# PSUM banks given out by the schedule in a fused Nyström attention and squared-ReLU MLP kernel: all eight banks in four tiles, one buffer for the squares, a stored table of priorities, the first inverse's last steps side by side

## The chip, the cores and the metric

The kernel runs on one core of one Trainium2 chip. The metric is the device time in microseconds (us) of one execution. The kernel before takes 254.74 us, the median of three runs (254.6 to 255.81). Names of engines: PE is TensorE (PEld its weight loads), ACT is ScalarE, DVE is VectorE, POOL is GpSimd, SP is SyncE.

## The reference, cut to what matters

```python
# q, k, v: (8, 8, 576, 64); w_in: (512, 2048); w_out: (2048, 512)
q_lm, k_lm = means of 18 consecutive rows of q and k          # 32 landmarks
A, Bm, C = sm(q, k_lm), sm(q_lm, k_lm), sm(q_lm, k)           # softmaxes
Z = Bm^T / (norms of Bm)
for _ in range(6):
    Z = 2 * Z - Z @ Bm @ Z                                    # iterated inverse
x = A @ Z @ C @ v                                             # -> (4608, 512)
h = x @ w_in;  r = maximum(h, 0);  out = (r * r) @ w_out      # -> (4608, 512)
```

## The kernel before

The kernel folds Z, C and v into w_in (G = (Z C v) w_in for each of the eight batches), so the MLP's first product is AT,G. Each step is an `Op` with an engine, a duration, what it reads and writes, and the PSUM banks that it takes. A list scheduler in the kernel orders all Ops by a model of the chip, and the program is emitted in that order. There are eight banks of 512 f32 columns. The kernel before has three rings: "h", two tiles of two banks each, and "n" and "o", two tiles of one bank each. Every entry of a ring is a tile of its own to the framework:

```python
RINGS = {"h": 2, "n": 2, "o": 2}

def bank(tag, key, shape, dt=F32):
    PS[key] = psum.tile(shape, dt, tag=tag, bufs=Plan.RINGS[tag], name=tag)
    return PS[key]
```

The two dense steps, with their evictions (cut):

```python
def in_mm(e, hk=hk, f=f):                  # h <- AT,G: two banks of 288 columns
    t = bank("h", hk, [P, 2, 512])
    ...
# ACT: r = relu(h), 576 columns over both banks, in one instruction;  DVE: gT = r * r
# PE:  o += gT[f]^T w_out[f], 16 steps of 512 columns into one bank of ring "o"
# ACT or DVE: osb = copy of that bank;  SP: store
```

The softmax here doesn't subtract the row's maximum and nothing guards it: scores larger than these inputs give would overflow.

## Time and profile before

| | kernel before |
|---|---|
| time, median | 254.74 us |
| span from first to last instruction | 253.2 us |
| PE busy | 95% |
| last quarter of w_in lands, its G group starts | 30.82, 30.86 us |
| last matmul ends | 249.6 us |

First, the shares of the chain that ended last:

```profile
PE 77%; DMA 9%; DVE 6%; POOL 3%; issue 2%; ACT 1%; POOLq 0%
```

ACT has 1%: PE almost never waits for an eviction. Second, the end of the timeline, with start, length, engine, line, operation, tiles and count:

```profile
241.19 8.40 PE L1112 MATMUL o<-w_out_bf,gT 128*128 128x512 bf16 x54
...
243.12 0.58 ACT L323 COPY o<-o 128x512 f32<-128x512 f32 x1 [3.40 <-PE o L1112]
...
246.68 0.58 ACT L323 COPY o<-o 128x512 f32<-128x512 f32 x1 [2.98 <-PE o L1112]
248.15 0.37 ACT L323 COPY o<-o 128x256 f32<-128x256 f32 x1 [0.88 <-PE o L1112]
```

PE runs 8.40 us of output matmuls without a gap, while ACT copies out the bank just finished three times. PE writes the other bank of the ring meanwhile.

### The profile page before, as it was taken

How to read it: one execution, taken by the hardware profiler on the slowest of the kernel's cores; microseconds unless marked ns; L12 is line 12 of the kernel's file. 1: busy time of each engine (PE TensorE's matmuls, PEld its weight loads, DVE VectorE, ACT ScalarE, POOL GpSimd, SP SyncE). 2: the span in 40 equal slices, each digit the busy share in tenths (PEclk: the TensorE clock that was granted, in tenths of full speed). 3: DMA queues.
4: the chain of work that ended last, by engine and by line, in shares of the span. 5: the costliest groups of instructions: out<-in, count | busy, mean ns of one | idle time of the engine just before them, and what ended most of it. 6: DMA issues, size and time to landing. Idle time of an engine off the chain costs nothing.

```text
span 253.2 us, 6580 instructions
## 1 busy us (share of the span) xinstructions
PE 239.9 (95%) x2666; PEld 143.9 (57%) x2701; DVE 174.4 (69%) x487; ACT 164.3 (65%) x282; POOL 29.1 (11%) x51
## 2 busy tenths in 40 slices
PE   8776999999999999999999999999999999999994
PEld 7553775456644656565645565467466644565453
DVE  2774789769966898799897799979866762253000
ACT  3586898567832887677865985679688744474211
POOL 7822200012003000300220030010000000000000
PEclk9995999999999999999999999999999999999999
DMA  7999999999999999799599949997110131301233
GB/s 145 192 206 205 204 206 206 163 165 185 196 112 218 147 229 166 133 202 225 110 159 230 197 58 220 196 177 134 44 41 3 44 83 41 85 0 41 85 83 83
DMA packets 57054, 35.59 MB, mean 141 GB/s; under 512 B 29760, under 2 KB 52544, under 8 KB 57024
## 3 DMA queue, kind: packets, MB, share of 16 engines
q0 software_dynamic: 22672, 18.06, 47.6%
q1 hardware_dynamic: 34352, 17.11, 33.2%
q8 instruction: 21, 0.34, 0.5%
q14 instruction: 9, 0.07, 0.1%
HBM read 36.70 MB, written 9.44 MB: 182 GB/s over the span
## 4 chain that ended last, share of the span: by engine, by line
PE 77%; DMA 9%; DVE 6%; POOL 3%; issue 2%; ACT 1%; POOLq 0%
PE o L1112 39%; PE h L315 12%; PE h L1044 11%; DMA w_in_bf<-in_moe_w_in_dram 8%; PE o L1099 6%; PE h L982 2%; DVE gT L1058 2%; PE n L842 1%; PE n L794 1%; PE n L890 1%; DVE G L325 1%; POOL w_in_bf L397 1%; POOL qraw L390 1%; ACT r L1055 1%; DVE o L325 1%
## 5 line engine op out<-in xcount | busy, mean ns | idle before, releaser
L1112 PE MATMUL o<-w_out_bf,gT 128*128 128x512 bf16 (+1 forms) x494 | 125.1, 372 | 1.9 <-issue 0.6
L1055 ACT ACTIVATE r<-h 128x576 bf16<-128x576 f32 x128 | 78.8, 651 | 20.9 <-PE h L315 18.7
L1058 DVE TENSOR_TENSOR gT<-r 128x576 bf16<-128x576 bf16 x128 | 56.6, 452 | 20.2 <-ACT r L1055 18.2
L1112 PEld LDWEIGHTS <-gT 128*128 128x128 bf16 x528 | 48.1, 98 | 39.2 <-issue 6.0
L1044 PE MATMUL h<-AT,G 128*128 128x288 bf16 x256 | 67.1, 288 | 0.8 <-DVE G L325 0.4
L315 PE MATMUL h<-AT,G 128*128 128x288 bf16 x256 | 67.0, 288 | 0.0
L323 ACT COPY o<-o 128x512 f32<-128x512 f32 (+1 forms) x27 | 15.4, 570 | 35.7 <-PE o L1112 26.4
L315 PEld LDWEIGHTS <-G 128*128 128x128 bf16 x256 | 25.2, 98 | 12.3 <-issue 0.3
L1044 PEld LDWEIGHTS <-G 128*128 128x128 bf16 x256 | 25.1, 98 | 11.4 <-DVE G L325 1.3
L323 ACT CAST G<-h 128x1024 bf16<-128x1024 f32 x17 | 17.2, 1018 | 6.4 <-PE h L982 5.4
L325 DVE CAST G<-h 128x1024 bf16<-128x1024 f32 x13 | 15.9, 1222 | 7.3 <-PE h L315 6.4
L483 POOL COPY gate<-qT 1x1 bf16<-1x1 bf16 x6 | 1.9, 316 | 124.1 <-DMA qT<-qraw 102.9
L807 DVE SCALAR_TENSOR_TENSOR st<-st,n 128x128 bf16<-128x128 bf16 x35 | 9.9, 284 | 7.6 <-PE n L794 7.6
L1099 PE MATMUL o<-w_out_bf,gT 128*64 128x512 bf16 x64 | 14.6, 380 | 0.0
L1101 PE MATMUL o<-w_out_bf,gT 128*64 128x512 bf16 x64 | 14.6, 380 | 0.0
L935 ACT ACTIVATE Ra<-h 128x576 f32<-128x576 f32 x16 | 10.3, 652 | 3.9 <-PE h L315 3.7
L462 DVE TENSOR_TENSOR Pd<-st,ones_d 128x256 bf16<-128x256 bf16 x42 | 12.1, 288 | 0.9
L946 DVE TENSOR_TENSOR AT<-Ea,Ra 128x576 bf16<-128x576 bf16 x16 | 11.7, 753 | 1.2 <-ACT Ra L939 1.2
L849 ACT ACTIVATE EC<-n 96x512 bf16<-96x512 f32 x21 | 12.0, 609 | 0.6 <-PE n L842 0.6
L923 ACT ACTIVATE Ea<-h 128x576 bf16<-128x576 f32 x16 | 9.9, 659 | 3.9 <-PE h L824 3.9
L794 PEld LDWEIGHTS <-Pd 128*128 128x128 bf16 x84 | 7.9, 97 | 6.9 <-DVE Pd L462 1.4
L1099 PEld LDWEIGHTS <-gT 128*64 128x64 bf16 x64 | 6.7, 110 | 7.1 <-issue 1.3
(174 smaller groups left out, 286.8 us busy)
## 6 DMA issues: line engine op xcount, KB each, us to landing
vraw<-in_v_dram POOLq DMA_DIRECT2D x8, 576.0 KB, 7.9
out_dram<-o SPq DMA_DIRECT2D x23, 192.0 KB, 2.5
kraw<-in_k_dram POOLq DMA_DIRECT2D x7, 576.0 KB, 10.1
qraw<-in_q_dram POOLq DMA_DIRECT2D x7, 576.0 KB, 13.4
out_dram<-o SPq DMA_DIRECT2D x24, 128.0 KB, 2.4
w_in_bf<-in_moe_w_in_dram POOLq DMA_DIRECT2D x4, 512.0 KB, 15.2
w_out_bf<-in_moe_w_out_dram POOLq DMA_DIRECT2D x4, 512.0 KB, 21.7
out_dram<-o SPq DMA_DIRECT2D x23, 64.0 KB, 2.2
```

Of the source, the lines that this page charges most:

```text
L315: nc.tensor.add_instruction(mybir.InstMatmult(start_tensor_calc=start, stop_tensor_calc=stop, is_transpose=transpose, ldweights=False, til ...
L323: nc.scalar.copy(dst, src)
L325: ENG[e].tensor_copy(dst, src)
L462: nc.vector.tensor_tensor(dst[:], src.unsqueeze(2).to_broadcast([P, 2, NG, M]), ones_d[:].unsqueeze(1).to_broadcast([P, 2, NG, M]), ALU.mult)
L849: nc.scalar.activation(EC[:, x, :, :, :, :].rearrange("p c i g m -> p (i g) c m"), PS[sc][0:TP, :, :].rearrange("p y (c m) -> p y c m", c= ...
L946: add(("DVE", dve_ns(S)), lambda e, i=i: nc.vector.tensor_tensor(AT[:, i, :], Ea[:, i, :, :].rearrange("p c t -> p (c t)"), Ra[:, i, :, :] ...
L1044: (again if j else nc.tensor.matmul)(t[:, j, 0:HALF], lhsT=G[:, i, f * P:(f + 1) * P], rhs=AT[:, i, j * HALF:(j + 1) * HALF], start=(i == ...
L1055: add(("ACT", act_ns(S)), lambda e, hk=hk, r=r: nc.scalar.activation(r.rearrange("p (j t) -> p j t", j=2), PS[hk][:, :, 0:HALF], AF.Relu), ...
L1058: add(("DVE", dve_ns(S, 2)), lambda e, r=r, f=f: nc.vector.tensor_tensor(gTs[z][:, f, :], r[:], r[:], ALU.mult), reads=[("r", rn)], writes ...
L1099: nc.tensor.matmul(t[0:64, :], lhsT=gTs[0][:, f, 4 * P:S], rhs=w_out_bf[:, f, :], start=(f == 0), stop=(f == NF - 1))
L1101: nc.tensor.matmul(t[64:P, :], lhsT=gTs[1][:, f, 0:64], rhs=w_out_bf[:, f, :], start=(f == 0), stop=(f == NF - 1))
L1112: nc.tensor.matmul(PS[ok][:, 0:hi - lo], lhsT=gTs[z][:, f, x0:x0 + P], rhs=w_out_bf[:, f, lo:hi], start=(f == f0), stop=(f == f1 - 1))
```

## The change

Its intent: let the schedule give out the eight banks freely (up to three two-bank tiles, three "n" and three "o" at a time, any that fit), replace 700 random rounds at build time by a stored table of annealed priorities, keep the squares of two batches in one buffer so that the row tiles that straddle two batches need one matmul per step, run the last steps of the first inverse side by side, and set dummy matmuls at more places of the front end. The diff, cut to what the argument touches (the table, most of the first inverse and the order of loads are left out):

```diff
-    RINGS = {"h": 2, "n": 2, "o": 2}
+    KINDS = {"h": (3, 2), "n": (3, 1), "o": (3, 1)}
+    NBANKS = 8
...
+    def take(self, rn, t, busy):
+        if self.KINDS[rn][1] == 2:
+            b = next(b for b in range(0, self.NBANKS, 2) if max(busy[b], busy[b + 1]) <= t)
+            return (b, b + 1)
+        return (min((busy[b ^ 1] <= t, busy[b], b) for b in range(2, self.NBANKS) if busy[b] <= t)[2],)
...
-    def bank(tag, key, shape, dt=F32):
-        PS[key] = psum.tile(shape, dt, tag=tag, bufs=Plan.RINGS[tag], name=tag)
+    pairs = [psum.tile([P, 2, 512], F32, name="ps%d" % i) for i in range(Plan.NBANKS // 2)]
+
+    def bank(key, shape, dt=F32):
+        b = plan.place[key]
+        t = pairs[b[0] // 2]
+        ...
+        if len(b) == 1:
+            ...
+            t = t[:, b[0] % 2, 0:n]
...
-            blocks((A, "u", 5), Ys[4], us[0], yk(4) + [("u", 4)], at(0.44), busy=1, dim=D)
+            blocks((A, "yy"), Ys[4], Ys[5], yk(4) + yk(5), at(0.42))
...
-    gTs = [sb.tile([P, NF, S], BF16, name="gT%d" % i) for i in range(2)]
+    gT = sb.tile([P, NF, 2 * S], BF16, name="gT")
...
-        end, log = self.search(700)
+        end, log = self.schedule(self.shifts(len(self.ops)))
```

## The prediction

> **What bounds the kernel now.** I first read the busy shares and the slices: PE is at 95% and at 9 in every slice from the fourth to the last but one, so TensorE is the bound, and only the ends are loose. In the slices PEclk falls to 5 once, in the fourth (19 to 25 us), and DMA is at 9 from the second slice on.
>
> ```profile
> PE 239.9 (95%) x2666; PEld 143.9 (57%) x2701; DVE 174.4 (69%) x487; ACT 164.3 (65%) x282; POOL 29.1 (11%) x51
> ...
> PE   8776999999999999999999999999999999999994
> ...
> PEclk9995999999999999999999999999999999999999
> DMA  7999999999999999799599949997110131301233
> ```
>
> Then the chain of work that ended last, in its first 50 us. The first batch's attention is not on it. It consists of the issuing of loads, then the fourth quarter of w_in, which lands at 30.82, and the G matmul that uses it, 0.04 us later; from there on it is PE.
>
> ```profile
> 9.65 0.71 POOL w_in_bf L397
> 10.37 20.45 DMA w_in_bf<-in_moe_w_in_dram
> 30.82 0.04 issue
> 30.86 0.41 PE h L982 x8
> ```
>
> So I cut the span there. Columns: stretch, its length, then busy us of PE, PEld, DVE, ACT, POOL, clock, DMA share, GB/s.
>
> ```profile
> 0.00:31.00 31.00, 24.12 (x483) 18.41 (x484) 18.28 (x72) 19.49 (x37) 14.98 (x29) 0.89 1.16 190
> 31.00:249.50 218.50, 215.66 (x2191) 125.51 (x2217) 156.16 (x416) 144.47 (x245) 14.10 (x22) 1.00 0.78 135
> 249.50:253.20 3.70, 0.09 (x1) 0.00 (x0) 0.00 (x0) 0.37 (x1) 0.00 (x0) 1.00 0.29 81
> ```
>
> Before 31 us PE idles 6.9 us, but the DMA engines never do. From 31 to 249.5 PE idles 2.8 us. The last 3.7 us are the last copy and store. Time = 30.8 (load) + dense PE work + 3.7; the time exceeds the span by 1.5 us (254.74 against 253.2).
>
> A finer look at the dense part, in the timeline of PE: a 512-column matmul starts 216 ns before its successor (median of 441 pairs). Where the successor uses another tile shape of the array it is longer: 39.92 to 40.23 and 41.02 to 41.33.
>
> ```profile
> 39.92 0.38 PE L1112 MATMUL o<-w_out_bf,gT 128*128 128x512 bf16 x1
> 40.23 0.56 PE L890 MATMUL n<-v,EC 96*32 96x65 bf16 x48
> ...
> 41.02 0.38 PE L1112 MATMUL o<-w_out_bf,gT 128*128 128x512 bf16 x1
> 41.33 0.44 PE L824 MATMUL h<-qT,kdup 64*32 64x288 bf16 x16
> ```
>
> Over 15 such pairs the median is 309 ns, so a change of tile shape costs 309 - 216 = 93 ns; after a 288-column matmul it is 216 - 123 = 93 ns too.
>
> **What the Trainium skill says.** "TensorEngine Tiling (Array Packing)", Key Properties: changing the tiling mode, not just the tile, drains TensorE. The trace agrees and gives the price, 93 ns. "TensorE: Matmul & The Clock Gate", Part 1: the clock is at half or full, decided over windows of about 3.4 us of activity. The trace has one half-clock stretch, 18.6 to 25.5 us, 6.83 us or two such windows. The same page, Part 2, says that weight loads are pulled ahead of matmuls in flight. The trace agrees: eight loads for the second half of a G pair are issued at 48.54 to 48.57, and their matmuls start at 48.74, right behind the first half's (48.52); the "no weight load" form of before still shows loads here. So splitting the G pairs into separate instructions should cost nothing. "PSUM — Partial Sum Buffer", Specifications: eight banks of 2 KiB; before fixes them as rings (two double banks, two and two single), after allots the same eight freely.
>
> **The change part by part.**
>
> *First inverse.* The chain at the start, in the timeline of PE:
>
> ```profile
> 19.47 0.29 PE L657 MATMUL n<-cvb,Z4T 32*32 32x64 bf16 x8
> 20.49 0.29 PE L657 MATMUL n<-u,Y 32*32 32x64 bf16 x8 [0.73 <-DVE u L325]
> 21.17 0.25 PE L970 MATMUL h<-Y,u 32*64 32x32 bf16 x8 [0.39 <-DVE u L664]
> 21.88 0.63 PE L982 MATMUL n<-w_in_bf,WT 64*32 64x512 bf16 x8 [0.45 <-ACT WT L323]
> ```
>
> The step u,Y (20.49 to 21.17, 0.68 us) goes; a product Y4 Y5 is made beside the other branch instead. The order of after also puts q's second means before its transposes (0.5 us earlier) and gives the C·v sums their own bank, so that they don't wait for the exponential that reads the shared one (a 0.17 us wait at 16.48). But v is now loaded after the first quarter of w_in: 14.04 becomes about 16.6, since a quarter takes 2.5 us (landings at 28.19 and 30.82). My estimate for the first G matmul is 20.3 in place of 21.88. This 1.5 us does not reach the end by itself: the same ten loads stand before w_in's fourth quarter, in another order, and DMA is saturated, so it still lands at about 30.8.
>
> *Work moved ahead of that landing.* This does reach the end. I counted PE's instructions in the program of each kernel, from the first G matmul to the last group of G of batch 0. Before has 24 of AT,G (288 columns, 122.5 ns) and 36 pairs of means and transposes of k and q (69 ns); after has 28 and 48. That is 4 x 0.1225 + 12 x 0.069 = 1.32 us more, less 0.11 us of one fold that comes later: 1.2 us. It fits: the second-to-last quarter of w_in lands at 28.2, then G 0.3, four matmuls 0.5 and 24 k pairs 1.65 end at 30.75. ACT has seven relus of 0.65 us to do in that time, which it can.
>
> *Both squares in one buffer.* The 64-row tiles of four batch pairs were done as two 128x64 matmuls per step; now it is one of 128x128. 64 steps of about 217.5 ns become 64 of 216: 0.1 us. Their tile shape no longer changes.
>
> *Tile shape changes.* In the two programs, from the first G on: 65 before, 57 after, 8 x 0.093 = 0.75 us.
>
> *Sum.* With each kind's spacing, PE's work from the last G group on is 216.3 us before and 214.35 after: 1.95 us less (1.2 + 0.75). Before took from 30.86 to the last matmul's issue at 249.4, 218.5 us, so 2.2 us were stalls and gaps; the single ones that I find without a missing record are 0.1 to 0.3 us each, about 1.5 us in all. Free banks (three double, three and three single at most) and an annealed order may save a third to a half: I take 0.7. Gain 2.65 us, less 0.3 for the rivals below: 254.74 - 2.35 = 252.4 us.
>
> **The rivals.**
> 1. *The front end pays in full.* If the load did not bind, G at 20.3 would add 1.5 us: about 250.9. The chain of waits speaks against it: 0.04 us between landing and use.
> 2. *The clock goes to half again, now later.* PE has only some 5.5 us of work from 20.3 to 28.2, and the stretch from 15.2 to 18.6, 73% busy, was followed by half clock. If 28.9 to 32.3 ran at half clock, the 24 k pairs (69 to about 107 ns) and AT,G matmuls would cost about 1.4 us: 253.8. For warmth speak the added dummy matmuls (13 more), but they stand before 22 us. I give it three in ten.
> 3. *A new wait for v of batch 1.* It is loaded behind all of w_out now: 30.8 + 4 x 2.5 + 2.9 = 43.8, plus the DVE copy of 0.95 us, against its use on PE, which my count puts at 45.0. Before it landed at 38.74, use at 40.23. A late copy could cost up to 1 us: 253.4.
> 4. *Banks do nothing,* because PE hardly waits for them: 253.1.
>
> **Range and chances.** 1 alone reaches 250.9; 2 and 3 together 254.5. Eight in ten: 250.8 to 254.0. Faster by over 2% needs 249.65, thus 5.1 us, of which the dense part cannot give more than 1.95 + 2.2 and the load's landing hides the rest: 0.06. Slower by over 2% would need a race of stalls that nothing here shows: 0.01.
>
> **What would show it right or wrong.** The last quarter of w_in should land at 30.5 to 31.2 us, with its G matmul right behind; the first G matmul near 20.3; PE's last matmul near 247.2; the tail 3.7; a change of tile shape still 93 ns. Wrong: the last G group well after its load (2, or ACT late); w_in landing by 29 us (1); a PE gap of over 0.5 us at 44 to 47 (3); stalls after 31 us that grow above 2.2 us, or a longer tail.

## More of the kernel before

The framework puts in the semaphore waits by itself. It orders accesses of different engines that overlap on a tile: a matmul that writes a tile waits for the copy that still reads it.

## The result, and the profile after

| | before | after |
|---|---|---|
| time, median of four runs | 255.28 us (254.60 to 257.01) | 286.39 us (285.51 to 287.44) |
| span of the profiled run | 253.2 us | 285.3 us |
| last quarter of w_in lands | 30.82 us | 30.64 us |
| the last G group of batch 0 starts | 30.86 us | 37.62 us |
| last matmul ends | 249.59 us | 281.64 us |

The four runs of the kernel before are the three named at the start and one more. The ratio is 1.1209, 95% interval 1.1133 to 1.1285. Ratios in this document are the mean time of one kernel's fast runs over that of the other's fast runs of the same rounds, so not quite the ratio of the medians quoted. One slow run of the kernel before (258.76 us, in the rounds of x1 to x3) is left out of the ratios.

The changed kernel is 12% slower, far outside the predicted range. Its page, in the order of the prediction's first fence, with the chain's shares last:

```profile
PE 251.2 (88%) x2621; PEld 145.9 (51%) x2658; DVE 174.2 (61%) x479; ACT 166.3 (58%) x287; POOL 28.9 (10%) x51
...
PE   7777889789989988899998899998987997899984
...
PEclk9975999999999999999999999999999999999999
...
PE 70%; DVE 13%; ACT 9%; issue 4%; DMA 2%; another core or an unknown queue 0%; DVEq 0%; ACTq 0%; POOLq 0%
```

The loss is not in one place. The row of PE, which was all 9 from the fourth slice on, has 7s and 8s to the end, and in the chain DVE and ACT have gone from 7% together to 22%. The stretches (columns as in the prediction), cut at the last G group and at the last matmul:

```profile
31.00:37.62 6.62, 4.65 (x90) 3.54 (x88) 3.39 (x8) 3.67 (x7) 0.00 (x0) 1.00 1.24 207
37.62:281.64 244.02, 222.13 (x2101) 124.71 (x2134) 155.47 (x410) 146.47 (x248) 14.01 (x22) 1.00 0.65 116
281.64:285.30 3.66, 0.00 (x0) 0.00 (x0) 0.00 (x0) 0.37 (x1) 0.00 (x0) 0.88 0.15 42
```

The front end is 6.76 us later (37.62 against 30.86), although the load that had set it landed when expected. The dense part takes 244.02 us in place of 218.73 (30.86 to 249.59), 25.3 us more. Together that is 32.1 us, the whole difference of the spans. The tail, 3.66 us, is as before.

What does PE wait for? The waits of the output matmuls (total us, times, longest), where the kernel before had only four "issue" waits of 0.6 us together:

```profile
PE ps L1178 <- ACT o L387: 5.9, 9, 0.7
...
PE ps L1178 <- DVE o L389: 1.8, 3, 0.8
PE ps L1178 <- DVE st L881: 1.7, 5, 0.4
```

An output matmul reads gT and w_out. It needs nothing of `st`, which is a step of another batch's inverse, nor of `o`, the copy of a finished output tile. The timeline at a place like the one shown of the kernel before:

```profile
269.76 1.24 PE L1178 MATMUL ps<-w_out_bf,gT 128*128 128x512 bf16 x5
...
271.04 0.58 ACT L387 COPY o<-ps 128x512 f32<-128x512 f32 x1 [3.95 <-PE ps L1178]
...
271.68 4.70 PE L1178 MATMUL ps<-w_out_bf,gT 128*128 128x512 bf16 x21 [0.67 <-ACT o L387]
...
274.68 0.58 ACT L387 COPY o<-ps 128x512 f32<-128x512 f32 x1 [3.05 <-PE ps L1178]
```

PE ends a tile, ACT copies it (0.58), and only then does PE begin the next tile, though that lies in another bank. The next copy, at 274.68, falls inside 4.70 us of matmuls that do not stop. So it depends on which banks the two tiles have. The front end shows the same:

```profile
16.39 0.22 PE L731 MATMUL ps<-Z,Y 32*32 32x32 bf16 x8 [0.23 <-ACT EC L923]
...
17.02 0.22 PE L731 MATMUL ps<-Y 32*32 32x32 bf16 x8 [0.41 <-ACT EC L923]
```

These are steps of the inverse, the longest chain at the start, waiting for an exponential of C, of which they read nothing.

The built program explains it. In the framework's record of dependences, a wait of this kind reads (matmul into the second bank of ps1, copy out of the first):

```
InstMatmult -> InstTensorCopy (sync): tensor overlap on 'ps1_64' (WAR)
```

I matched every wait of PE on ACT or DVE in the program with the instruction awaited. In the kernel before none is for an instruction that touches only another bank. In the changed kernel 92 are (41 on ACT, 51 on DVE), each between the two banks of one two-bank tile. I call them false waits below: the data need no such order, and they come from tiles, not from banks. Of the stalls that I could match to the program after 31 us, 23.8 us in all, 20.4 us in 40 stalls stand at false waits alone.

The Trainium skill bears on whether the chip needs such a wait: "PSUM — Partial Sum Buffer", section "PSUM bank collisions raise a hardware error", has the rule "Semaphore-guard PSUM by bank × quadrant (by bank is the simple version), not by address." The kernel before agrees: during 8.40 us of matmuls into one bank or the other, ACT read the bank that PE was not writing, three times. A two-bank tile is a coarser guard than a bank.

### The profile page after: what moved, and what is told of

Read it like the earlier page. It is cut to its first block, busy times and chain, and to the rows that moved or that the text cites. A ratio compares the mean times of both kernels' runs of the same rounds, so it can differ in the third digit from the quotient of the medians.

```text
span 285.3 us, 6505 instructions
## 1 busy us (share of the span) xinstructions
PE 251.2 (88%) x2621; PEld 145.9 (51%) x2658; DVE 174.2 (61%) x479; ACT 166.3 (58%) x287; POOL 28.9 (10%) x51
## 4 chain that ended last, share of the span: by engine, by line
PE 70%; DVE 13%; ACT 9%; issue 4%; DMA 2%; another core or an unknown queue 0%; DVEq 0%; ACTq 0%; POOLq 0%
PE ps L1178 39%; PE ps L379 11%; PE ps L1122 9%; ACT o L387 3%; DMA kraw<-in_k_dram 2%; PE ps L1060 2%; ACT r L1134 2%; DVE gT L1137 2%; ACT EC L923 1%; PE ps L916 1%; PE ps L868 1%; DVE st L881 1%; DVE AT L1021 1%; DVE o L1192 1%; PE ps L898 1%
## 5 line engine op out<-in xcount | busy, mean ns | idle before, releaser
L1178 PE MATMUL ps<-w_out_bf,gT 128*128 128x512 bf16 (+1 forms) x557 | 143.8, 373 | 18.3 <-ACT o L387 5.9
L1134 ACT ACTIVATE r<-ps 128x576 bf16<-128x576 f32 x128 | 76.5, 658 | 13.7 <-PE ps L379 9.8
L1122 PE MATMUL ps<-AT,G 128*128 128x288 bf16 x256 | 66.6, 288 | 1.0 <-DVE G L389 0.3
L379 PE MATMUL ps<-AT,G 128*128 128x288 bf16 x256 | 66.5, 288 | 0.0
L387 ACT COPY o<-ps 128x512 f32<-128x512 f32 (+1 forms) x30 | 17.0, 571 | 56.4 <-PE ps L1178 52.2
L387 ACT CAST G<-ps 128x1024 bf16<-128x1024 f32 (+2 forms) x22 | 19.5, 941 | 6.3 <-PE ps L1060 6.3
L389 DVE CAST G<-ps 128x1024 bf16<-128x1024 f32 (+2 forms) x14 | 14.9, 1067 | 11.6 <-PE ps L1060 9.9
L881 DVE SCALAR_TENSOR_TENSOR st<-st,ps 128x128 bf16<-128x128 bf16 x35 | 10.0, 285 | 17.7 <-PE ps L868 11.9
L923 ACT ACTIVATE EC<-ps 96x512 bf16<-96x512 f32 x24 | 13.5, 594 | 3.0 <-PE ps L916 2.4
L1010 ACT ACTIVATE Ra<-ps 128x576 f32<-128x576 f32 x16 | 10.3, 648 | 5.3 <-PE ps L379 5.1
L1060 PE MATMUL ps<-w_in_bf,WT 64*32 64x512 bf16 (+1 forms) x264 | 10.6, 390 | 0.4 <-ACT qpad L387 0.4
```

Source lines behind the costliest of these rows:

```text
L379: nc.tensor.add_instruction(mybir.InstMatmult(start_tensor_calc=start, stop_tensor_calc=stop, is_transpose=transpose, ldweights=False, til ...
L387: nc.scalar.copy(dst, src)
L389: ENG[e].tensor_copy(dst, src)
L881: add(("DVE", 290.0), lambda e, st=st, sn=sn, nv=nv: nc.vector.scalar_tensor_tensor(out=sn.rearrange("p i z m -> p (i z m)"), in0=st.rearr ...
L923: nc.scalar.activation(EC[:, x, :, :, :, :].rearrange("p c i g m -> p (i g) c m"), PS[sc][0:TP, :, :].rearrange("p y (c m) -> p y c m", c= ...
L1060: nc.tensor.matmul(ts[i][M * g:M * g + M, lo:hi], lhsT=WT[64 * i:64 * i + 64, g, :], rhs=w_in_bf[64 * i:64 * i + 64, g, n * 512 + lo:n * 5 ...
```

## The experiments

Four theories. **Theory 1**: the false waits cost the 32 us. **Theory 2**: the stored order suits the model, not the chip. **Theory 3**: the one buffer for the squares makes DVE wait for PE (a wait of up to 10.9 us of the squares on output matmuls is new). **Theory 4**: cold clock and dummy matmuls in the front end (half clock from 18.2 to 28.4 us, against 18.6 to 25.5 before).

All results in one table. False waits are counted in the built program. "Last G" is the start of the last G group of batch 0. "Stalls" are my count of the time after 31 us by which the start of a matmul is 60 ns or more later than its kind's spacing (216 ns at 512 columns, 123 at 288, 93 more at a change of tile shape). Gaps as long as one missing record are left out, but some 2 us of other artefacts remain where records are missing. Each ratio is to the kernel before on the same chip.

| run | false waits of PE | median us | ratio (95%) | last G | last matmul ends | stalls us |
|---|---|---|---|---|---|---|
| before | 0 | 255.28 | | 30.86 | 249.59 | 3.3 |
| after | 92 | 286.39 | 1.121 (1.113 to 1.129) | 37.62 | 281.64 | 32.1 |
| x1_own_tiles | 0 | 256.62 | 1.000 (0.992 to 1.009) | 31.20 | 251.51 | 5.2 |
| x2_order_kept_shared | 80 | 284.87 | 1.114 (1.105 to 1.122) | 34.23 | 279.50 | 29.7 |
| x3_before_shared | 70 | 288.02 | 1.124 (1.116 to 1.132) | 38.31 | 283.30 | 30.2 |
| x6_only_o_shared | 40 | 279.17 | 1.089 (1.086 to 1.093) | 33.45 | 273.84 | 24.4 |
| x5_no_dummies | 0 | 257.21 | 1.002 (0.996 to 1.007) | 31.73 | 252.04 | 5.2 |
| x7_annealed | 0 | 255.99 | 0.998 (0.994 to 1.002) | 33.47 | 251.28 | 1.4 |
| x8_before_table | 0 | 255.59 | 0.998 (0.994 to 1.003) | 30.90 | 249.41 | 1.2 |
| x1_again | 0 | 257.50 | 1.006 (1.002 to 1.010) | 29.93 | 250.78 | 2.6 |
| x9_front_kept | 0 | 255.32 | 0.999 (0.994 to 1.003) | with the third, 31.15 | 250.14 | 4.2 |
| x10_eight_tiles | 0 | 255.09 | 0.998 (0.991 to 1.004) | 30.61 | 249.35 | 1.9 |
| x11_before_split | 138, between halves | 257.48 | 1.005 (1.001 to 1.008) | 31.05 | 251.29 | 1.7 |
| x12_eight_again | 0 | 255.19 | 0.995 (0.992 to 0.999) | 30.91 | 249.66 | |

All gave correct results. The 138 waits of x11 lie between the halves of one tile of a ring. The next tile of that ring takes both banks, so it needs both copies; but it is its first matmul, into the first bank, that waits for the copy of the second, which that matmul alone doesn't need. The unsplit kernel before waits there for the one instruction that reads both.

### x1_own_tiles and x2_order_kept_shared: the same order, with and without the shared tile

An instruction that reads two banks needs one tile for them, so x1 keeps two two-bank tiles (banks 0 to 3) and makes banks 4 to 7 four tiles. The schedule differs from the changed kernel's, because it has fewer places to choose from.

```diff
-    KINDS = {"h": (3, 2), "n": (3, 1), "o": (3, 1)}
+    KINDS = {"h": (2, 2), "n": (3, 1), "o": (3, 1)}       # two-bank tiles in banks 0-3, singles in 4-7
+    singles = [psum.tile([P, 512], F32, name="pb%d" % i) for i in range(4, 8)]
```

> The changed kernel with every single PSUM bank as a tile of its own: two tiles of two banks (banks 0 to 3) for what needs two at once, banks 4 to 7 as four tiles of 512. Scheduler, table, dummy matmuls, one buffer for the squares, side-by-side inverse all stay; only the table's rows now meet another bank plan. In the built program no wait of TensorE, ScalarE or VectorE is for an instruction that touched only the neighbouring bank (92 on TensorE in the changed kernel). Theory 1 (the loss of 32 us is the waits between neighbours in a two-bank tile, some 24 us in the dense part and the rest in the front end): 250 to 258 us, dense-part stalls back under 6 us. Theory 2 (the annealed order itself does not suit the chip): stays over 275 us. Theory 3 (one buffer for the squares): stays over 275, with the VectorE wait of 10.9 us on TensorE still there and TensorE idle around it. Theory 4 (cold clock in the front end): about 280, half clock still granted to 28 us.

x2 has x1's schedule. In the two built programs every engine has the same instructions in the same order, at the same PSUM addresses, but for the waits. x2 declares the four single banks as two tiles again:

```diff
-    singles = [psum.tile([P, 512], F32, name="pb%d" % i) for i in range(4, 8)]
+    singles = [t[:, c, :] for t in [psum.tile([P, 2, 512], F32, name="pb%d" % i) for i in (4, 6)] for c in range(2)]
```

> Instruction for instruction the order and the banks of x1_own_tiles, but banks 4 to 7 are declared as two tiles of two banks and sliced, so the only difference is which waits the framework adds: 80 TensorE waits for the other bank of the pair (30 on ScalarE, 50 on VectorE) where x1_own_tiles has none. Theory 1: at least 265 us, and the difference to x1_own_tiles is the false waits' price. Theories 2, 3 and 4: within 2% of x1_own_tiles.

Measured: 256.62 and 284.87 us. The output matmuls' group of x1 (busy, mean ns, then idle time before them):

```profile
L1179 PE MATMUL pb<-w_out_bf,gT 128*128 128x512 bf16 (+1 forms) x557 | 139.9, 373 | 2.0 <-issue 0.8
```

The same group of x2, where only the declaration differs:

```profile
L1179 PE MATMUL pb<-w_out_bf,gT 128*128 128x512 bf16 (+1 forms) x560 | 146.5, 373 | 17.3 <-ACT o L388 4.0
```

Four banks declared as two tiles cost 28 us: the last G group 3.0 us later and the dense part 25.0 us longer. Theories 2, 3 and 4 gave both kernels the same time and are refuted as causes of this loss. For theory 3 there is also x1's own 256.62 us: it has the one buffer, and in its waits the squares on DVE stand for output matmuls for 0.2 us only. That wait was an effect, not a cause.

### x3_before_shared and x6_only_o_shared: the false waits alone, added to the kernel before

Nothing of the change is in these. x3 takes the two banks of ring "n" out of one two-bank tile and those of ring "o" out of another; x6 does so for "o" only. The order is the one of the kernel before.

```diff
-    PS[key] = psum.tile(shape, dt, tag=tag, bufs=Plan.RINGS[tag], name=tag)
+    t = twos[tag][:, turn[tag] % 2, 0:n];  turn[tag] += 1       # twos: psum.tile([P, 2, 512]) for "n" and "o"
```

> The kernel before, with its own order and nothing of the change, except that the two banks of the n ring are slices of one two-bank tile and the two of the o ring of another: 70 TensorE waits (45 on ScalarE, 25 on VectorE) for the neighbouring bank where the kernel before has none. Theory 1: clearly slower than 255 us, 270 to 290, with o matmuls standing some 0.8 us for the copy of the bank just finished. Theories 2, 3 and 4: no change, 254 to 257 us.

> The kernel before, with only the two banks of the o ring as slices of one two-bank tile (the n ring as it was): 40 TensorE waits for the neighbouring bank instead of 70. In x3_before_shared the idle time of output matmuls put down to copies of o was 10.3 (ScalarE) and 5.7 us (VectorE). If each false wait is a price of its own: about 256 + 16 = 272 us, between before and x3_before_shared (288), with some 26 stalls of 0.6 to 1.0 us ahead of the first matmul of an output tile. If a total time near 288 or near 256 comes out, the price isn't per wait.

Measured: 288.02 and 279.17 us. So the false waits of x3 by themselves make the kernel before as slow as the changed one. They also prolong the half clock in the profiled runs: 23.9 us of it in x3 and 13.7 in x6, against 6.8 in the kernel before, with nothing else changed. My figure for x6 was wrong: I expected 272. It came from the idle time in this view of x3, which reads the same in x6:

```profile
PE two_o L1127 <- ACT o L338: 10.3, 18, 0.9
PE two_o L1127 <- DVE o L340: 5.7, 8, 1.0
```

16.0 us of idle, but x6's profiled run is 24.3 us longer than the kernel before's. Three things were missing. First, idle is not the loss. In the timeline of the changed kernel above, the last of the five matmuls starts at 269.76 + 4 x 0.216 = 270.62 and the next at 271.68: 1.06 us where 0.22 is regular, so 0.84 us are lost, while the view says 0.67 of idle. The rest is the tail of the last matmul (0.373 long, 0.216 to its successor), in which the page still counts PE as busy. Summed from start to start, the 26 waits of this view cost 19.9 us. This is one reason why PE looks busier after the change (251.2 against 239.9 us) with less to do. Second, two more stalls, 0.9 and 0.8 us, were put down to other lines. Third, the last G group starts 2.6 us later (33.45 against 30.86), which no wait of an output matmul shows. Together 24.2 us.

### x5_no_dummies: theory 4 and the front end

```diff
-        if plan.now.fill:
+        if False:                                           # in idle(): no dummy matmuls
```

> x1_own_tiles, same order, without the eight dummy matmuls that the changed kernel sets ahead of the first inverse's last steps, the first G group and the first AT,G group (they stood behind the same wait as the work they lead, so they ran after the idle time and ahead of the work, 19.97 to 23.06 us there). If they cost time: first G group some 1 to 1.5 us earlier than 23.06 (about 21.8). If they bought the clock: the half-clock stretch grows from one record window (3.4 us) to two or three and the first G group is later than 23.06. In both cases the total within 1% of x1_own_tiles (256.6), because the last G group waits for the fourth quarter of w_in (30.58 us) and not for the front end.

Measured: 257.21 us, as x1. The edit took away thirteen dummy matmuls, not eight: four stood at 12.2 to 12.8 us in x1, just ahead of where x5's half clock begins (12.91), and nine at 20.0 to 23.1. A part of each side of the expectation came true: the first G group was earlier, and the half clock longer (four windows). The stretch from 12 to 26.5 us, x1 and then x5; the third number from the end is the granted clock:

```profile
12.00:26.50 14.50, 11.61 (x275) 7.25 (x275) 8.84 (x37) 10.40 (x23) 3.43 (x5) 0.88 1.29 204
```

```profile
12.00:26.50 14.50, 11.78 (x255) 8.19 (x256) 8.70 (x37) 10.06 (x21) 3.79 (x5) 0.53 1.29 205
```

Without the dummies the clock is at half for 13.65 us in place of 3.4. The first G group starts at 22.18, earlier than x1's 23.06 by the clock on the wall, but v also landed 1.36 us earlier in that run (15.79 against 17.15), so counted from v it is 0.5 us later. The last G group starts 0.53 us later than in x1 and the last matmul ends 0.53 us later: the dense part is 220.31 us in both. In this pair, the later front end was paid in full and no more. Single runs decide this clock differently, though (x1_again held it at full throughout), so one pair of traces doesn't size what dummies are worth. The record has the mean clock of every run: 0.972 to 0.992 in the four of x5 (mean 0.979), 0.978 to 1.0 in the ten of x1 and x1_again (0.990). So the dummies seem to buy clock, but they ran on different chips, and the time did not show it.

### x7_annealed, x8_before_table, x1_again, x9_front_kept: is the order worth anything?

x1 has a table made for another bank plan. x7 replaces it by one searched for x1's plan with the kernel's own scheduler; x8 gives such a table to the kernel before; x9 searches with the first 122 steps held to x1's. Only the string of the table differs (and the call in x8).

```diff
-    "_kifEfPk#i`q#~XfPjF2fPjF2fPjFBw0!LK=GcTw3xm*acD7r)u|3E|?W>i|#1YHMcY%OszY04YG&)mLh+-9>?AvdR3UC<^KPWP&Mg0m*l0h"
+    (another table of 1797 entries)
```

> x1_own_tiles with a new table of priorities, searched (some 130,000 schedules) for its own bank plan with the kernel's own scheduler; the table of the changed kernel was made for the other bank plan. The scheduler's clock says 246.4 us where it says 249.5 for x1_own_tiles, 245.7 for the changed kernel and 248.2 for the kernel before. If that clock holds for differences (it has no false waits to miss here): 3 us less than x1_own_tiles, 252 to 254 us, some 1% under the kernel before, and the prediction's 252.4 is what the change's other parts are worth once the waits are gone. If the order was never the point: 256 to 257 like x1_own_tiles.

> The kernel before with nothing of the change but a searched table (80,000 schedules) in place of the 700 random rounds at build time. The scheduler's clock says 247.75 us, against 248.24 with the 700 rounds: 0.5 us less, so 255 to 257 us, no difference that the rounds can show. More than 1.5 us less would mean that a table alone is the part that pays.

> x1_own_tiles unchanged, for a comparison with x7_annealed on one chip with more rounds: 256 to 257 us, within 0.5% of the kernel before.

> As x7_annealed, a table searched for the bank plan of x1_own_tiles, but the first 122 steps of the schedule are held to those of x1_own_tiles (which kept the full clock in its front end but for 0 to 3.4 us, where x7_annealed had 13.7 us of half clock and its last G group 3.5 us after the load). The scheduler's clock says 246.7. From the traces: x7_annealed took 217.8 us from the last G group to the last matmul. If that holds with a last G group right behind the load (29.9 to 31 us), the span is 30.4 + 217.8 + 3.6 = 251.8, the time 253 to 254 us and the ratio to the kernel before about 0.99. If the work merely shifts (what is not done ahead of the last G group has to be done after it): dense part near 220 and 255.5 to 257 us, as x1_own_tiles.

Measured: 255.99, 255.59, 257.50 and 255.32 us; only x1_again differs from the kernel before, by 0.6%. The 3 us that the scheduler's clock promised x7 are about half there: its median is 1.5 us below that of x1_again on the same chip. The dense part of x7 shrank to 217.8 us, but its last G group came 3.5 us after the load, with 13.65 us of half clock before it:

```profile
PEclk9965899999999999999999999999999999999999
```

x9 has the front end of x1, and then its dense part is 219.0 us from the start of its last two G groups. So my hope for x9 (253 to 254 us) fell, and the second branch, "the work merely shifts" (255.5 to 257), fits better, though the time lies just below it. No table that I tried moved the time of a kernel without false waits by as much as 1%.

### x10_eight_tiles, x11_before_split, x12_eight_again: the changed kernel's own order without false waits

x1 leaves one hole: its schedule isn't the changed kernel's. x10 keeps that schedule exactly and makes all eight banks tiles of their own. An eviction of two banks becomes two.

```diff
-    pairs = [psum.tile([P, 2, 512], F32, name="ps%d" % i) for i in range(Plan.NBANKS // 2)]
+    ones8 = [psum.tile([P, 512], F32, name="pb%d" % i) for i in range(Plan.NBANKS)]
...
-            add(("ACT", act_ns(S)), lambda e, hk=hk, r=r: nc.scalar.activation(...PS[hk][:, :, 0:HALF]...
+            (the same on each bank in turn, and so for every eviction of two banks)
```

> The changed kernel with its own bank plan, table and order on TensorE, instruction for instruction, but all eight banks are tiles of their own. What was one eviction of a two-bank tile becomes two of one bank each (188 more ScalarE instructions), since an instruction can't read two tiles: an exponential or relu of 576 columns (653 ns) becomes two of 288, some 160 ns more, about 30 us of ScalarE in all (166 to 196 us of a span of 255, not the bound, but each result comes 0.16 us later in an order that does not expect it). No wait for a neighbouring bank is left (92 before). Theory 1: 255 to 264 us, whatever is above 256 being the price of the split. Theory 2 (the order of the changed kernel itself is bad on the chip): over 275.

x11 is the control: the kernel before with the same split of evictions.

> Control for x10_eight_tiles: the kernel before with the same split of every eviction of a two-bank tile into two, nothing else. Gives the price of the split in an order that did not expect it: 256 to 264 us. x10_eight_tiles less this is what the rest of the change does without its false waits; under theory 1 between -3 and +3 us.

Measured: 255.09 us for x10 and 257.48 for x11. The page's first row and the output matmuls of x10:

```profile
PE 244.6 (97%) x2658; PEld 144.0 (57%) x2658; DVE 175.1 (69%) x493; ACT 173.2 (68%) x469; POOL 28.6 (11%) x51
```

```profile
L1195 PE MATMUL pb<-w_out_bf,gT 128*128 128x512 bf16 (+1 forms) x592 | 145.1, 374 | 0.0
```

No idle before 592 output matmuls, where the changed kernel had 18.3 us before those recorded. Same order on PE, same banks, another declaration and the split that it forces: 286.4 becomes 255.1 us. The split itself doesn't explain the gain: x11, with a split, is not faster than the kernel before. Theory 2 is refuted for the changed kernel's own order too. The split was cheaper than I had expected: ACT is busy 173.2 us, not 196.

> x10_eight_tiles unchanged with more rounds, to see whether it beats the kernel before (0.9975, 0.991 to 1.0039 there). The prediction's gain of 2.35 us less the price of the split (x11_before_split: 1.0045, about 1.1 us) would be 0.995: 254.5 to 255.5 us with an interval that lies below 1. If the other parts of the change are worth nothing: 1.000 to 1.005.

Measured: 255.19 us, ratio 0.9954 (0.9924 to 0.9985), inside "same" at 2%. This 0.5% can't be put down to the banks or the order, for two reasons. Seven of the eight runs of the kernel before in this ratio are those of x10's rounds. And the granted clock differs: 0.993 to 1.0 in x12's six runs, 0.966 to 0.978 in those eight. In the experiments' 43 runs of the kernel before (one of them slow), span and clock go together: 252.8 to 253.2 us at 0.986 to 0.987, 254.3 to 255.1 at 0.973, 255.5 to 257.0 at 0.964 to 0.966. x12's spans, 252.6 to 253.8, are no shorter than those of the kernel before at 0.987. The better clock may come from the added dummy matmuls, but no run here separates that.

Against x11, through the kernel before, x12 is 0.9954 / 1.0045 = 0.991, some 2.3 us; the two were not timed against each other directly, x11 has the 138 waits between halves that x12 lacks, and its clock was lower too (0.973 to 0.986).

## Why the prediction was wrong

I go by its steps.

- **The frame, load + dense part + 3.7.** The load (30.64) and the tail (3.66) came as predicted. That the last G group follows the load at once failed: it came 7.0 us after. This was on the list of signs that would show me wrong, but the false waits were not among the causes named there. x10, without false waits, has the group 0.54 us after the load (30.61 against 30.07).
- **First G group near 20.3.** It came at 25.35. Without false waits it was 22.2 (x10) and, where the clock stayed full, 20.98 (x1_again). That it does not pay by itself held: x1_again started its last G group 0.04 us after the load, nearly 9 us after the first.
- **Work ahead of the load, mid tiles, tile shapes (1.2 + 0.1 + 0.75 us).** The counts came true (484 records of AT,G from the last G group on in x10, which is 512 less the 28 counted), and a change of shape still costs 93 ns (309 against 216). Their gain doesn't stand out singly. x10's dense part is 218.74 us, as the kernel before's 218.73, but that of x11, with the split, is 220.24 and thus 1.5 us longer, so the change might be worth up to 1.5 us in the dense part. This is not shown: a part of x11's 1.5 us can be its waits between halves, which x10 doesn't have.
- **"Free banks (three double, three and three single at most) and an annealed order may save a third to a half: I take 0.7."** This is the step that failed. The premise was my sentence "before fixes them as rings (two double banks, two and two single), after allots the same eight freely": I took a bank for the unit in which waits are made. x2 and x3 show that the unit is the tile. Allotting banks freely out of four two-bank tiles added 92 waits, and in place of a saving of 0.7 the stalls after 31 us went from about 3 to 32 us (a sign that the prediction had listed). The clue was in the diff: `pairs` holds four tiles where the rings held six. I also quoted the page on PSUM for the eight banks and didn't ask who guards them.
- **The rivals.** Rival 1 (the front end pays in full) is refuted by x1_again. Rival 2 (half clock from 28.9 to 32.3) did not come as named; the half clock came earlier and longer, 18.2 to 28.4 us, as a part of the front end's delay. How much of the 6.8 us is clock and how much is false waits was not separated, but x2 against x1 shows 3.0 us of such delay with nothing but waits added (half clock 6.8 us in x2's profiled run, 3.4 in x1's). Rival 3 (v of batch 1) did not show: in x10 no stall of 60 ns or more lies between 40 and 92 us. Rival 4 (banks do nothing: 253.1) fits in that own tiles brought no clear gain, but its figure was not reached: x1 took 256.62, x10 255.09 us.
- **The chances.** I gave 0.01 to a loss of over 2%, since "a race of stalls that nothing here shows" seemed needed. The profile of before could not show it: those waits weren't in its program. They could be read from the built program of the changed kernel, which I had and did not search for waits.
- **Slips in its sums, which decide nothing.** The profiled run of the kernel before took 254.92 us, so time exceeds span by 1.7 us and not 1.5. The 0.1 us of the squares is not in the 1.95. 30.8 + 4 x 2.5 + 2.9 is 43.7. Rivals 2 and 3 together, as each is priced singly, make 252.4 + 1.4 + 1.0 = 254.8.

What stays open: the shares of false waits, half clock and dummies in the 6.8 us of the front end, and what each part of the change is worth singly. Without false waits all of them together moved the time by less than 1%, which is no more than what the granted clock moves in the kernel before.

## What to carry to other kernels

Ask in which unit the framework makes its waits before you slice a buffer: two accumulators that different engines use at the same time should be two tiles, even where memory is given out by hand, and a scheduler's model has to book that same unit. When a change replaces separate tiles by slices of shared ones, list the new waits of the built program and look for any that no data asks for; the profile of the old kernel can't show them. Price a stall from start to start: the idle time on the page left out a fifth here (16.0 of 19.9 us in x6). And before you read anything from a difference below 1%, compare the granted clock of the runs.

## What the Trainium skill lacked or had wrong

- No page says that a framework which orders accesses by tile makes banks of one tile wait for each other. "PSUM — Partial Sum Buffer" gives the rule for guarding by bank, but not what a coarser guard costs: 80 false waits cost 28 us (x2 against x1), and the one timed above 0.84 us.
- "TensorEngine Tiling (Array Packing)", Key Properties, says that a change of mode drains TensorE, without a price: 93 ns here, before and after (309 against 216 ns).
- "ScalarE: Activation LUTs", section "What ACT_TABLE_LOAD costs", says that back-to-back ACTIVATEs overlap by about 93 ns. Splitting 128 relus of 576 columns into 256 of 288 raised ScalarE's busy time for them from 76.5 us (after) to 84.0 (x10), which is 59 ns for each added instruction. For x11 against the kernel before it is 78.8 to 87.0, 64 ns. An estimate from the page's figures, 186 ns of start (immediate scale and bias) less the 93 that overlap, is 93 ns for each; I had expected 160.
- "TensorE: Matmul & The Clock Gate", Part 1: the table of the two states has the clock fall after an idle window of about 3.4 us. The section on a second failure mode there lets frequent short idles do it too, without saying how much idle that takes. Here the clock was at half from 18.6 us on in the kernel before, after the stretch from 15.2 to 18.6 that was 73% busy, so a window need not be idle. Nor does the busy share alone decide it: in x1_again the stretch from 16.05 to 19.46 was 70% busy and the clock stayed full. Two runs of one program (x1_own_tiles and x1_again) had 3.4 and 0 us of half clock.
